# Output tiles of a fused attention and maxout kernel divided in two, with a new order of work

## The chip, the cores and the metric

The kernel runs on one core of one Trainium2 chip. Time is device time in microseconds of one execution; several executions give a median. The core has five engines with a queue each: PE (matrix multiply), ACT and DVE (elementwise, both can read the matmul results), POOL (elementwise, and here the issuer of nearly all loads) and SP (the issuer of stores). Matmul results lie in PSUM, which has eight banks of 128 partitions by 512 float32.

## The reference

Eight batches of eight heads go through an attention with 32 memory slots, and the result goes through a maxout layer.

```python
# q, k, v: (8, 8, 576, 64); phi: (8, 8, 576, 32)
a = softmax(phi, axis=2)                      # over the 576 positions
k_m = einsum('bhsm,bhsd->bhmd', a, k)
v_m = einsum('bhsm,bhsd->bhmd', a, v)
attn = softmax(q @ k_m^T / 8, axis=-1)        # over the 32 slots
x = (attn @ v_m)                              # to (4608, 512)
h = max(x @ w1, x @ w2, x @ w3)               # w1, w2, w3: (512, 768)
out = h @ w_out                               # w_out: (768, 512), out: (4608, 512) float32
```

## The kernel before, in words

**The algebra.** `x` is never formed. Per batch, `v_m` is folded into the weights: `wp = v_m (w1 - w3 | w2 - w3)` and `wp3 = v_m w3 w_out`. Then `h = w3-part + max(0, attn wp_1, attn wp_2)`, so a tile of the output is six matmuls of the hidden part with `w_out` and two of `attn` with `wp3`.

**Orders by hand.** Nothing is scheduled by a tool at build time: a string of tokens (line 602 on) is walked, and each token `n@b` issues one piece of work for batch `b`. Each engine runs its instructions in exactly that order. A `!` swaps which engine, ACT or DVE, copies the result out of PSUM. A second string (line 145) gives in order the PSUM bank that each piece takes, one digit for each; pieces that need two banks take the digit and the next one up. Semaphores hold an instruction until its inputs are there and its bank has been read.

**The tokens, per batch.**

| token | what it does | engines |
|---|---|---|
| L0, L1, L2, L3 | load phi, k, v, q (line 575) | POOL issues, DMA moves |
| r0, r1 | pack k, v into one buffer (line 102) | POOL |
| E | exp of phi (line 232) | ACT |
| B | `a^T (k, v, 1)`, 72 small matmuls (line 245) | PE |
| N, K | divide by the sum, transpose (lines 269, 299) | DVE, PE, copy on DVE or ACT |
| Q0, Q1 | transpose q (line 313) | DVE |
| S | scores and their exp (line 327) | PE, ACT |
| a, s, c, m, X | softmax over slots: transpose, sum, reciprocal, multiply, transpose back | DVE, POOL for m |
| D0, D1, D2, D3 | fold a block of 512 weight columns; D3 is `wp3` (line 427 on) | PE, copy on ACT or DVE |
| F0 to F11 | hidden tile: four matmuls 128x288; an even one is copied with max(0, .), the odd one behind it is joined by max on DVE (line 463) | PE, ACT, DVE |
| T0 to T4 | output tile, 128 rows by 512: eight matmuls, a copy, a store (line 495) | PE, ACT or DVE, SP |
| V0, V1, V2 | `w1 - w3`, `w2 - w3` in place, once (line 215) | DVE |

T4 exists for odd batches alone: its 128 rows are the last 64 of the batch before and the first 64 of this one. Its six matmuls with `w_out` span all 128 columns of the array; the two with `attn` become four narrow ones (128x64), two for either batch, since `wp3` differs.

**Shapes on the PE.** F, T, K and the warm-up matmuls use the whole 128x128 array. B and D use tiles of 64x32, S tiles of 32x32, the narrow part of T4 tiles of 128x64.

**Depth of buffers.** phi and q: two tiles each. k and v: two each. `wp`, `attn`, the hidden tile: two each. The output tile: six. So the load of k for batch b + 2 waits for the pack of batch b, and a load of q for b + 2 for the transposes of b.

**Around batch 2.** In the old order B@2 comes after the tiles T3@0, T0@0, T1@0, T2@0 and all twelve F@1; then D3@1, N@2, Q1@2, T0@1, K@2, T2@1, Q0@2, S@2.

Of the kernel before, what the change touches and what calls it, by code (L numbers as in the profile page):

```python
# [15 lines left out]
def kernel(  # L16
# [138 lines left out]
    def one_bank():  # L155
        return psum[:, int(next(banks))]
# [306 lines left out]
    def ffn1(b, n, swap):  # L463
        s = st[b]
        ft, w = n // 2, n % 2
        if b // 2 not in hts:
            hts[b // 2] = work.tile([P, FT, 2 * S], BF16, name="hT")
        hT, attn = hts[b // 2], attns[b // 2]
        acc = two_banks()
        for g in range(NG):  # L470
            for h in range(2):
                c0 = (b % 2) * S + h * SH
                nc.tensor.matmul(  # L473
                    acc[:, h, 0:SH],
                    lhsT=wps[b][:, g, w * DF + ft * P : w * DF + (ft + 1) * P],
                    rhs=attn[:, g, c0 : c0 + SH],
                    start=(g == 0),
                    stop=(g == NG - 1),
                )
# [15 lines left out]
    def ffn2(b, t, swap):


        hT, attn = hts[b // 2], attns[b // 2]
        c0 = S - HP if t == 4 else (b % 2) * (S + HP) + t * P
        if b == B - 1 and t == 3:  # L500
            return ffn2_last(b, c0)
# [9 lines left out]
        for g in range(NG):  # L511
            if t < 4:
                nc.tensor.matmul(  # L513
                    po,
                    lhsT=attn[:, g, c0 : c0 + P],
                    rhs=wp3s[b][:, g, :],
                    start=False,
                    stop=(g == NG - 1),
                )
            else:  # L520
                for u in range(2):
                    nc.tensor.matmul(  # L522
                        po[HP * u : HP * (u + 1)],
                        lhsT=attn[:, g, c0 + HP * u : c0 + HP * (u + 1)],
                        rhs=wp3s[b - 1 + u][:, g, :],
                        start=False,
                        stop=(g == NG - 1),
                        tile_position=(0, HP * u),
                    )
# [70 lines left out]


    for w in """
        E@0 H0@0 H2@0 L3@0 Z25@0 B0@0 I@0 N0@0 Z2@0 K0@0! Q0@0 Q1@0 Z9@0 S@0 Z2@0 M0@0 M1@0
        R0@0 Y2@0 G0@0 R1@0 W0@0 Y3@0 W1@0 W2@0 Z6@0 O1@0 H3@0 O3@0 O2@0 H1@0 X1@0 B1@0 X0@0 N1@0
        K1@0 O0@0 Y0@0 D1@0! D0@0! D3@0 F8@0 F10@0 F2@0 V0@0 F6@0 F0@0! Y1@0 D2@0 D4@0 F4@0
# [5 lines left out]
        X1@2 D0@2 T3@1 Q0@3 L3@4 X0@2 Q1@3 T1@1 F0@2 F4@2 F8@2 F6@2 F9@2 E@3 F7@2 r1@3 F5@2  # L611
        F10@2 F1@2 B@3 L1@4 D3@2 N@3 L0@5 F2@2 F11@2 E@4 F3@2 L1@5 K@3 r1@4 L2@5 T2@2! S@3 T3@2
        a0@3 s0@3 c0@3 m0@3 D0@3 D2@3 a1@3 s1@3 c1@3 X0@3 D1@3! Q0@4 m1@3 T1@2 L3@5 L2@6 T0@2!
        X1@3 F10@3 r0@4 F2@3 F4@3 E@5 Q1@4 r0@5 F5@3 F3@3 L1@6 F8@3 B@4 N@4 D3@3 F9@3 F6@3
        F11@3 L0@6 K@4 F0@3 F7@3 F1@3 S@4 a0@4 T4@3! s0@4 a1@4 D0@4 c0@4 s1@4 r1@5 c1@4 D3@4
        m0@4 X0@4 Q0@5 T0@3! D1@4! D2@4 B@5 T3@3 m1@4 X1@4 L0@7 F10@4 Q1@5 N@5 F8@4 K@5 F6@4
        F9@4 S@5 F7@4 L3@6 F2@4 F4@4 a0@5 L1@7 a1@5 F0@4 s0@5 r1@6 F3@4 D0@5 r0@6 s1@5 c1@5 E@6
        D3@5 m1@5 c0@5 F1@4 T1@3 L2@7 F11@4 L3@7 E@7 F5@4 m0@5 B@6 D1@5! D2@5 X1@5 N@6 T2@3!
        X0@5 F6@5 F8@5 Q0@6 Q1@6 K@6 F4@5 F9@5 S@6 F7@5 r0@7 a0@6 F2@5 a1@6 s0@6 c0@6 F0@5
        F10@5 m0@6 F1@5 s1@6 c1@6 F11@5 F5@5 T0@4! F3@5 X0@6 T2@4! r1@7 D0@6 D1@6! Q0@7 B@7  # L620
# [37 lines left out]
```

## Time and profile before

| | us |
|---|---|
| median of 3 runs | 165.57 (165.14 to 166.01) |
| the profiled execution | 165.42 |
| its span | 163.70 |
| PE busy | 153.0 |
| ACT busy | 100.5 |
| DVE busy | 90.4 |
| POOL busy | 69.7 |
| loads by POOL's queue, share of 16 DMA engines over the span | 68.7% |

Starts and durations are counted from the start of the span. An idle time is named with what ended it. A matmul's duration in the trace is that of its pipeline: 128x512 shows 380 ns, while one starts every 216 ns; 128x288 shows 286 ns and starts every 123. Some matmul records are missing: of 210 matmuls of line 504 the trace holds 193, and a missing one looks like idle time.

### The profile page before, as it was taken

To read this page: it belongs to the slowest core of one execution; us is meant where nothing else is said; L and a number is where in the kernel's file an instruction comes from. 1 tells how busy PE (TensorE), PEld (TensorE's weight loads), DVE (VectorE), ACT (ScalarE), POOL (GpSimd) and SP (SyncE) were. 2 spreads that over 40 slices of the span, in tenths; PEclk is the share of its full clock that TensorE was granted. 3 is DMA by queue.
4 is the path that set the end of the run, shared out by engine and by line. 5 is a ranking of instruction groups with operands and counts; after the bars stand their busy time and mean duration, and the time that the engine had idled before them with its cause. 6 is when DMAs were issued, how large, how long until landed. Compare 5 with 4: busy or idle time off the path is not lost.

```text
span 163.7 us, 4819 instructions
## 1 busy us (share of the span) xinstructions
PE 153.0 (93%) x2060; PEld 85.5 (52%) x2080; DVE 90.4 (55%) x181; ACT 100.5 (61%) x151; POOL 69.7 (43%) x72
## 2 busy tenths in 40 slices
PE   7987798999898999999999999999999999999990
PEld 2442444664376436753673575576553467744450
DVE  2023703898837765759399759879749228810000
ACT  4205335935496488778885989994658976323320
POOL 7275215100698276838939976755403200000000
PEclk9999999999999999999999999999999999999999
DMA  5999999999999999999999999997313230014333
GB/s 155 156 207 200 197 210 213 277 208 208 259 307 241 209 257 364 277 216 286 258 265 206 233 351 266 175 235 157 130 70 125 73 128 0 0 68 180 141 128 130
DMA packets 21974, 31.77 MB, mean 194 GB/s; under 512 B 1216, under 2 KB 16576, under 8 KB 21952
## 3 DMA queue, kind: packets, MB, share of 16 engines
q0 software_dynamic: 16080, 21.43, 68.7%
q1 hardware_dynamic: 5728, 9.90, 17.2%
q8 instruction: 16, 0.26, 0.6%
q10 hardware_dynamic: 144, 0.13, 0.2%
q14 instruction: 6, 0.05, 0.1%
HBM read 39.32 MB, written 9.44 MB: 298 GB/s over the span
## 4 chain that ended last, share of the span: by engine, by line
PE 65%; DMA 28%; POOL 2%; issue 2%; ACT 1%; POOLq 0%; ACTq 0%
PE psum L504 25%; PE psum L473 22%; DMA ph<-in_phi_dram 15%; DMA w_sb<-in_moe_w_dram 9%; PE psum L513 7%; DMA kvo<-in_k_dram 4%; PE psum L447 4%; PE psum L256 3%; PE psum L340 1%; POOL kvo L97 1%; PE psum L522 1%; PE psum L545 1%; ACT e L236 1%; PE psum L305 1%; POOL wo_sb L123 0%
## 5 line engine op out<-in xcount | busy, mean ns | idle before, releaser
L504 PE MATMUL psum<-wo_sb,hT 128*128 128x512 bf16 x193 | 49.7, 380 | 1.4 <-issue 0.6
L473 PE MATMUL psum<-attn,wp 128*128 128x288 bf16 x384 | 50.5, 286 | 0.1
L486 DVE TENSOR_TENSOR hT<-psum,h 128x576 bf16<-128x576 f32 x48 | 34.2, 749 | 18.2 <-PE psum L473 12.0
L473 PEld LDWEIGHTS <-wp 128*128 128x128 bf16 x384 | 36.7, 98 | 13.2 <-issue 1.9
L179 ACT COPY ot<-psum 128x512 f32<-128x512 f32 x35 | 20.7, 591 | 32.1 <-PE psum L513 25.2
L504 PEld LDWEIGHTS <-hT 128*128 128x128 bf16 x210 | 19.2, 98 | 24.1 <-issue 4.3
L103 POOL COPY kvr<-kvo 128x2304 bf16<-128x2304 bf16 x12 | 25.4, 2114 | 14.3 <-DMA kvo<-in_k_dram 7.9
L179 ACT CAST wp<-psum 128x1024 bf16<-128x1024 f32 (+1 forms) x31 | 29.3, 996 | 3.0 <-PE psum L447 2.1
L177 ACT ACTIVATE h<-psum 128x576 bf16<-128x576 f32 x47 | 28.4, 659 | 3.2 <-PE psum L473 3.1
L416 POOL TENSOR_TENSOR t<-t,sm 128x576 bf16<-128x576 bf16 x14 | 16.1, 1157 | 25.2 <-DVE sm L411 25.1
L513 PE MATMUL psum<-wp,attn 128*128 128x512 bf16 x62 | 18.4, 379 | 0.0
L166 PE MATMUL psum<-warm 128*128 128x512 bf16 x42 | 12.4, 450 | 1.4 <-DVE warm L135 1.2
L320 DVE STREAM_TRANSPOSE qT<-qq 128x576 f32<-128x576 f32 x16 | 11.7, 747 | 1.5 <-DMA qq<-in_q_dram 1.5
L349 ACT ACTIVATE e<-psum 128x576 bf16<-128x576 f32 x16 | 9.6, 652 | 3.8 <-PE psum L340 3.8
L236 ACT ACTIVATE e<-ph 128x1152 bf16<-128x1152 f32 (+1 forms) x9 | 9.6, 1065 | 2.6 <-DMA ph<-in_phi_dram 2.4
L402 DVE TENSOR_REDUCE sm<-t 128x18 f32<-128x576 bf16 x14 | 10.3, 738 | 0.2
L97 POOL DMA_DIRECT2D kvo<-in_v_dram x9 | 6.7, 747 | 7.2 <-PE psum L256 4.1
L513 PEld LDWEIGHTS <-attn 128*128 128x128 bf16 x62 | 6.1, 98 | 7.1
L394 DVE STREAM_TRANSPOSE t<-e 128x288 f32<-128x288 f32 x14 | 6.3, 464 | 6.2 <-ACT e L349 6.1
L562 DVE COPY ot<-psum 128x256 f32<-128x256 f32 x1 | 0.4, 425 | 15.4 <-PE psum L553 15.4
L256 PEld LDWEIGHTS <-e 64*32 64x32 bf16 x720 | 6.9, 90 | 3.4 <-issue 2.0
L166 PEld LDWEIGHTS <-warm 128*128 128x128 bf16 x44 | 4.6, 111 | 7.4 <-issue 3.5
(58 smaller groups left out, 116.4 us busy)
## 6 DMA issues: line engine op xcount, KB each, us to landing
out_dram<-ot SPq DMA_DIRECT2D x35, 256.0 KB, 5.5
qq<-in_q_dram POOLq DMA_DIRECT2D x8, 576.0 KB, 12.6
ph<-in_phi_dram POOLq DMA_DIRECT2D x7, 576.0 KB, 15.1
kvo<-in_k_dram POOLq DMA_DIRECT2D x7, 576.0 KB, 13.9
kvo<-in_v_dram POOLq DMA_DIRECT2D x7, 576.0 KB, 16.6
w_sb<-in_moe_w_dram POOLq DMA_DIRECT2D x3, 768.0 KB, 15.0
wo_sb<-in_moe_w_out_dram POOLq DMA_DIRECT2D x1, 768.0 KB, 10.7
ph<-in_phi_dram SPq DMA_DIRECT2D x2, 288.0 KB, 2.9
```

Source lines behind the costliest of these rows:

```text
L103: nc.gpsimd.tensor_copy(out=kvrs[b % 2][:, :, :, D * i : D * (i + 1)], in_=kvos[b % 2][:, 1 - i])
L166: nc.tensor.matmul(po[:, 0:BANK], lhsT=warm[:, 0:P], rhs=warm, start=True, stop=True)
L177: nc.scalar.activation(out=out_, in_=in_, func=AF.Relu)
L179: nc.scalar.copy(out=out_, in_=in_)
L236: nc.scalar.activation(out=s["e"][:, js], in_=loaded[b]["ph"][:, js], func=AF.Exp)
L256: nc.tensor.matmul(kvp[M * j : M * (j + 1), a, 0:nd], lhsT=s["e"][r, j, c, :], rhs={None: lambda: kvr[r, j, c, 0:nd], 0: lambda: k_and_one ...
L320: nc.vector.transpose(out=s["qT"][:, j].rearrange("p j c r e -> p (j c r e)").bitcast(FP32), in_=loaded[b]["q"][:, j].rearrange("p j c d - ...
L416: nc.gpsimd.tensor_tensor(out=t, in0=t, in1=s["sm", g].unsqueeze(2).to_broadcast([P, S // HP, R, 2]), op=ALU.mult,)
L473: nc.tensor.matmul(acc[:, h, 0:SH], lhsT=wps[b][:, g, w * DF + ft * P : w * DF + (ft + 1) * P], rhs=attn[:, g, c0 : c0 + SH], start=(g == ...
L486: nc.vector.tensor_tensor(out=hT[:, ft, (b % 2) * S : (b % 2 + 1) * S].rearrange("p (h n) -> p h n", h=2), in0=a, in1=s["h1", ft], op=ALU.max,
L504: nc.tensor.matmul(po, lhsT=hT[:, fc, c0 : c0 + P], rhs=wo_sb[:, fc, :], start=(n == 0), stop=False,)
L513: nc.tensor.matmul(po, lhsT=attn[:, g, c0 : c0 + P], rhs=wp3s[b][:, g, :], start=False, stop=(g == NG - 1),)
```

## The change

Three things change in the code, and with them both strings.

- A new token P issues the head of an output tile: its bank is taken, and the first three of the six matmuls with `w_out` run. The token T of the same tile later issues the other three and the two with `attn`, without taking a bank. 22 tiles are divided so; T4 and the last tile are not.
- In T4 the four narrow matmuls come first and open the accumulation, and the six wide ones follow and close it.
- The subtraction of `w3` is cut into the same four pieces as before, but one token issues one piece (V0, V1, V2, V4), where V1 issued two.
- The order of the tokens and the swaps are new behind D2@0; up to there they are the same. The banks are new throughout.

```diff
+    HEAD = 3
...
     def w_diff(n):
 
-        c, end = n * BANK, (n + 1) * BANK
-        while c < end:
-            e = min(end, (c // DF + 1) * DF)
-            nc.vector.tensor_tensor(
-                out=w12[:, :, c:e],
-                in0=w12[:, :, c:e],
-                in1=w_sb[:, :, 2, c % DF : c % DF + e - c],
-                op=ALU.subtract,
-            )
-            c = e
+        lo, end = FIRST[n]
+        nc.vector.tensor_tensor(
+            out=w12[:, :, lo:end],
+            in0=w12[:, :, lo:end],
+            in1=w_sb[:, :, 2, lo % DF : lo % DF + end - lo],
+            op=ALU.subtract,
+        )
...
+    heads = {}
+
+    def ffn2_head(b, t):
+
+        hT = hts[b // 2]
+        c0 = (b % 2) * (S + HP) + t * P
+        po = heads[b, t] = one_bank()
+        for n in range(HEAD):
+            fc = fts[b][n]
+            nc.tensor.matmul(
+                po,
+                lhsT=hT[:, fc, c0 : c0 + P],
+                rhs=wo_sb[:, fc, :],
+                start=(n == 0),
+                stop=False,
+            )
...
     def ffn2(b, t, swap):
...
-        po = one_bank()
-        for n, fc in enumerate(fts[b]):
+        po = heads[b, t] if (b, t) in heads else one_bank()
+
+        if t == 4:
+            for g in range(NG):
+                for u in range(2):
+                    nc.tensor.matmul(
+                        po[HP * u : HP * (u + 1)],
+                        lhsT=attn[:, g, c0 + HP * u : c0 + HP * (u + 1)],
+                        rhs=wp3s[b - 1 + u][:, g, :],
+                        start=(g == 0),
+                        stop=False,
+                        tile_position=(0, HP * u),
+                    )
+        for n in range(HEAD if (b, t) in heads else 0, FT):
+            fc = fts[b][n]
             nc.tensor.matmul(
                 po,
                 lhsT=hT[:, fc, c0 : c0 + P],
                 rhs=wo_sb[:, fc, :],
-                start=(n == 0),
-                stop=False,
+                start=(n == 0 and t < 4),
+                stop=(n == FT - 1 and t == 4),
             )
...
+            "P": lambda: ffn2_head(b, i),
```

The part of the order from batch 1's first B to the end of batch 2's scores, old and new, and the stretch around K@5 in the new one:

```diff
-        L0@1 V1@0 F1@0 E@1 F3@0 L1@1 F5@0 F9@0 F7@0 L3@1 F11@0 B0@1 T3@0 N0@1 K0@1! L2@1 Q1@1
-        L2@2 L1@2 Q0@1 L0@2 V2@0 T0@0! L3@2 S@1 T1@0 a0@1 s0@1 c0@1 m0@1 B1@1 N1@1 a1@1 L1@3
-        K1@1 s1@1 D0@1 D1@1! D2@1 c1@1 m1@1 X0@1 L3@3 r1@2 X1@1 T2@0! L2@3 F6@1 F10@1 F7@1 F2@1
-        F3@1 F4@1 F0@1 r0@2 E@2 F5@1 F1@1 F11@1 L0@3 L0@4 F8@1 L2@4 F9@1 B@2 D3@1 N@2 Q1@2
-        T0@1! K@2 T2@1! r0@3 Q0@2 S@2 a0@2 a1@2 s1@2 c1@2 m1@2 T4@1! D1@2! s0@2 D2@2 c0@2 m0@2
+        N1@0 K1@0 O0@0 Y0@0 D1@0! D0@0! D3@0 F8@0 F10@0 F2@0 V0@0 F6@0 F0@0! Y1@0 D2@0 L0@1
+        V2@0 L1@1 D4@0 V1@0 L3@1 F4@0 F3@0 L2@1 L1@2 F1@0 L2@2 F7@0 F5@0 F9@0 F11@0 P0@0 E@1
+        B0@1 N0@1 T3@0 K0@1! Q0@1 Q1@1 L0@2 T0@0! S@1 L3@2 P1@0 V4@0 B1@1 a0@1 T1@0 s0@1 L3@3
+        N1@1 c0@1 L2@3 a1@1 s1@1 K1@1 c1@1 m0@1 P2@0 X0@1 D1@1 D0@1 m1@1 D2@1 X1@1 T2@0! L1@3
+        r0@2 F2@1! F10@1 F0@1! F4@1 F8@1 F5@1 r1@2 F6@1 L0@3 E@2 F9@1 F11@1 L0@4 L1@4 F1@1 F7@1
+        P2@1 F3@1 B@2 N@2 D3@1 P3@1 P0@1 K@2! Q0@2 Q1@2 T0@1! S@2 a0@2 s0@2 c0@2 T4@1! m0@2
...
+        F8@3! F3@3 E@4 F4@3 F9@3 F5@3 F0@3 F7@3 B@4 D3@3 N@4 F1@3 P1@3 K@4 L1@6 L0@6 T1@3! r1@5
+        E@5 S@4 D2@4 L2@6 a0@4 T4@3! r0@5 s0@4 L0@7 a1@4 P0@3 D1@4! B@5 s1@4 c1@4 D0@4 L1@7
+        c0@4 Q1@5 m1@4 T0@3! N@5 Q0@5 K@5 P2@3 L2@7 X1@4 m0@4 S@5 X0@4 T2@3! F0@4 F2@4 a0@5
...
-        F9@6 F1@6 F3@7 T0@6! T0@7! T3@5 T2@7! T2@6! T1@6 T1@7 T3@6 T4@7! T3@7
+        P2@6 F1@7 F6@7 F7@7 T2@6 F4@7! T3@6! F8@7 T0@6! T1@6 F9@7 F5@7 F3@7 P0@7 T1@7! T0@7
+        T2@7 T4@7! T3@7
```

The string of banks changes with it:

```diff
-            00224460026701101401264026402640264026452063420643064206420642064562074206742064
-            20642064201640264102640264026402640264072406247026402640264024602406520462046204
-            62704267402640264124602416420642064206420642067676767670
+            60606026024506010445024062406246024602434403424206026420462406240723043240604602
+            46026402645260502624620640264024601642102461462624604624260462045260024062404206
+            12640264014206502402605220462406420462036040432402677670
```

More of the change, by code (lines that the diff above doesn't have):

```diff
@@ L493 @@
     osts = {}
[L495 to L501, printed above, removed]
-        po = one_bank()
-        for n, fc in enumerate(fts[b]):
+    heads = {}
[5 more added lines that the diff above has]
+            fc = fts[b][n]
             nc.tensor.matmul(
@@ L510, in ffn2 @@
             )
-        for g in range(NG):
-            if t < 4:
+    def ffn2(b, t, swap):
+        hT, attn = hts[b // 2], attns[b // 2]
+        c0 = S - HP if t == 4 else (b % 2) * (S + HP) + t * P
+        if b == B - 1 and t == 3:
+            return ffn2_last(b, c0)
+        po = heads[b, t] if (b, t) in heads else one_bank()
[19 more added lines that the diff above has]
+            )
+        if t < 4:
+            for g in range(NG):
                 nc.tensor.matmul(
@@ L519, in ffn2 @@
                 )
[L520 to L529, printed above, removed]
         ot = opool.tile([P, DM], FP32, name="ot")
@@ L603 @@
         E@0 H0@0 H2@0 L3@0 Z25@0 B0@0 I@0 N0@0 Z2@0 K0@0! Q0@0 Q1@0 Z9@0 S@0 Z2@0 M0@0 M1@0
-        R0@0 Y2@0 G0@0 R1@0 W0@0 Y3@0 W1@0 W2@0 Z6@0 O1@0 H3@0 O3@0 O2@0 H1@0 X1@0 B1@0 X0@0 N1@0
-        K1@0 O0@0 Y0@0 D1@0! D0@0! D3@0 F8@0 F10@0 F2@0 V0@0 F6@0 F0@0! Y1@0 D2@0 D4@0 F4@0
-        L0@1 V1@0 F1@0 E@1 F3@0 L1@1 F5@0 F9@0 F7@0 L3@1 F11@0 B0@1 T3@0 N0@1 K0@1! L2@1 Q1@1
-        L2@2 L1@2 Q0@1 L0@2 V2@0 T0@0! L3@2 S@1 T1@0 a0@1 s0@1 c0@1 m0@1 B1@1 N1@1 a1@1 L1@3
-        K1@1 s1@1 D0@1 D1@1! D2@1 c1@1 m1@1 X0@1 L3@3 r1@2 X1@1 T2@0! L2@3 F6@1 F10@1 F7@1 F2@1
@@ L609 @@
-        F3@1 F4@1 F0@1 r0@2 E@2 F5@1 F1@1 F11@1 L0@3 L0@4 F8@1 L2@4 F9@1 B@2 D3@1 N@2 Q1@2
-        T0@1! K@2 T2@1! r0@3 Q0@2 S@2 a0@2 a1@2 s1@2 c1@2 m1@2 T4@1! D1@2! s0@2 D2@2 c0@2 m0@2
[L611 to L620, printed above, removed]
@@ L621 @@
-        m1@6 N@7 X1@6 T2@5! K@7 T3@4 Q1@7 S@7 a0@7 F2@6 s0@7 a1@7 s1@7 c1@7 m1@7 c0@7 F4@6
-        T4@5! D3@6 D2@7 D0@7! T0@5! D3@7 D2@6 X1@7 m0@7 D1@7! T1@4 X0@7 F6@7 F3@6 T1@5 F4@7
-        F8@7 F0@7 F5@6 F10@6 F7@7 F9@7 F10@7 F5@7 F0@6 F11@7 F6@6 F1@7 F7@6 F2@7 F8@6 F11@6
-        F9@6 F1@6 F3@7 T0@6! T0@7! T3@5 T2@7! T2@6! T1@6 T1@7 T3@6 T4@7! T3@7
+        R0@0 Y2@0 G0@0 R1@0 W0@0 Y3@0 W1@0 W2@0 Z6@0 O1@0 H3@0 O3@0 O2@0 H1@0 X1@0 B1@0 X0@0
+        N1@0 K1@0 O0@0 Y0@0 D1@0! D0@0! D3@0 F8@0 F10@0 F2@0 V0@0 F6@0 F0@0! Y1@0 D2@0 L0@1
@@ new lines @@
+        V2@0 L1@1 D4@0 V1@0 L3@1 F4@0 F3@0 L2@1 L1@2 F1@0 L2@2 F7@0 F5@0 F9@0 F11@0 P0@0 E@1
[3 more added lines that the diff above has]
+        P2@1 F3@1 B@2 N@2 D3@1 P3@1 P0@1 K@2! Q0@2 Q1@2 T0@1! S@2 a0@2 s0@2 c0@2 T4@1! m0@2
+        a1@2 s1@2 c1@2 T2@1! D2@2 Q1@3 D0@2 D1@2! T3@1 m1@2 T1@1 X1@2 r1@3 L3@4 L2@4 X0@2 L2@5
@@ new lines @@
+        Q0@3 F4@2 F6@2 F0@2 F8@2 F7@2 r0@3 F1@2 F10@2 F5@2 E@3 F9@2 F11@2 F2@2 B@3 D3@2 N@3
+        F3@2 L0@5 P3@2 K@3 P0@2 L1@5 S@3 T0@2 a0@3 r0@4 s0@3 c0@3 a1@3 s1@3 P2@2 m0@3 c1@3 D2@3
+        m1@3 D1@3! L3@5 D0@3 T3@2! Q1@4 X0@3 X1@3 T2@2! Q0@4 T1@2 F10@3! r1@4 F2@3 F11@3 F6@3
+        F8@3! F3@3 E@4 F4@3 F9@3 F5@3 F0@3 F7@3 B@4 D3@3 N@4 F1@3 P1@3 K@4 L1@6 L0@6 T1@3! r1@5
+        E@5 S@4 D2@4 L2@6 a0@4 T4@3! r0@5 s0@4 L0@7 a1@4 P0@3 D1@4! B@5 s1@4 c1@4 D0@4 L1@7
+        c0@4 Q1@5 m1@4 T0@3! N@5 Q0@5 K@5 P2@3 L2@7 X1@4 m0@4 S@5 X0@4 T2@3! F0@4 F2@4 a0@5
@@ new lines @@
+        F4@4! F6@4 r1@6 a1@5 P3@3 L3@6 D1@5! r0@6 D3@4 s1@5 D3@5! T3@3 F10@4 s0@5 c1@5 F3@4
+        F8@4 c0@5 F11@4 F1@4 F7@4 F5@4 F9@4 m0@5 P1@4 P0@4 E@6 D0@5 m1@5 X0@5 B@6 D2@5 X1@5
+        T0@4 T1@4 N@6 F6@5 F0@5 F7@5 F1@5 F4@5! Q0@6 F2@5 r0@7 F10@5 r1@7 T3@4! Q1@6 F5@5 F8@5!
+        E@7 K@6! F9@5 T2@4! F3@5 S@6 F11@5 a1@6 B@7 L3@7 D2@6 N@7 a0@6 D0@6 T4@5! s0@6 K@7 Q1@7
+        P0@5 s1@6 D1@7! D3@7 c1@6 c0@6 D0@7 Q0@7 m1@6 T0@5! m0@6 P1@5 S@7 T1@5 X1@6 a0@7 a1@7
+        P3@5 X0@6 D2@7 D1@6! s0@7 c0@7 D3@6 s1@7 T3@5! m0@7 c1@7 F6@6 P2@5 m1@7 X0@7 X1@7 F10@6
@@ L625 @@
+        T2@5! F7@6 F10@7! F4@6 F0@7! F11@6 F8@6 F11@7 F0@6! F2@6 F5@6 F1@6 F3@6 F2@7! P3@6 F9@6
+        P2@6 F1@7 F6@7 F7@7 T2@6 F4@7! T3@6! F8@7 T0@6! T1@6 F9@7 F5@7 F3@7 P0@7 T1@7! T0@7
+        T2@7 T4@7! T3@7
     """.split():
```

## The prediction

> **What bounds the kernel now.** I read the busy table and the 40 slices first, then stages, then the PE's waits, then the chain in order of time.
>
> ```profile
> span 163.7 us, 4819 instructions
> PE 153.0 (93%) x2060; PEld 85.5 (52%) x2080; DVE 90.4 (55%) x181; ACT 100.5 (61%) x151; POOL 69.7 (43%) x72
> DMA  5999999999999999999999999997313230014333
> ```
>
> ```profile
> 0.00:26.60 26.60, 22.28 (x272) 10.28 (x275) 6.79 (x20) 8.87 (x14) 12.20 (x24) 1.00 1.07 189
> 26.60:52.30 25.70, 24.30 (x409) 14.75 (x413) 19.21 (x32) 17.81 (x28) 10.90 (x11) 1.00 1.17 249
> 52.30:115.30 63.00, 62.16 (x982) 36.20 (x992) 46.84 (x98) 49.56 (x72) 43.09 (x36) 1.00 1.12 247
> 115.30:160.00 44.70, 44.27 (x408) 24.25 (x410) 17.58 (x32) 23.88 (x37) 3.46 (x4) 1.00 0.26 98
> ```
>
> The columns after the stretch are PE, PEld, DVE, ACT and POOL busy, granted clock, DMA share and GB/s. Up to 26.6 us the PE waits for weights and fills with warm-up matmuls. From 52.3 to 160.0 it lacks 1.27 us in all (63.00 - 62.16 + 44.70 - 44.27), and those are mostly missing matmul records (193 of 210 of line 504 are in the trace). So after 52.3 us time can go down only by giving the PE less to do there. The clock is 1.00 throughout.
>
> ```profile
> PE psum L305 <- DVE kvn L280: 0.9, 2, 0.4
> PE psum L256 <- ACT e L236: 0.4, 1, 0.4
> PE psum L305 <- DVE kvn L290: 0.4, 1, 0.4
> PE psum L447 <- DVE kvt L183: 0.3, 1, 0.3
> ```
>
> ```profile
> 27.17 23.86 DMA ph<-in_phi_dram
> 51.05 1.17 ACT e L236
> 52.27 0.80 PE psum L256 x69
> ```
>
> After 27 us the PE's real waits are 0.43 us at 42.75 (K1@1), 0.32 at 43.30 (the fold behind it) and 0.41 at 52.27. The last decides: phi of batch 2 lands at 51.03, its exp (E@2) takes 1.17, and B@2 starts at 52.27 however early the PE is there. The two earlier waits are therefore already paid for by it: without them the PE would wait 1.16 at 52.27.
>
> **The change part by part.** Time outside the span is 165.42 - 163.70 = 1.72 us; the profiled 165.42 is 0.15 below the median 165.57. I sum against 165.42 and add 0.15 at the end.
>
> *Same work.* The split adds no matmul: a head of 3 and a rest of 3 + 2 are the old 8. The PE has 4162 instructions in both orders. The subtraction pieces (two of 1198 ns, two of 684 ns) are the same four; they stay in the DVE order ahead of the folds that read them. Priced at nothing: DVE is at 75% in that stage.
>
> *Front.* Up to D2@0 the tokens are the same and only banks differ; the fold D1@0 still waits for w1 (landed at 26.6). Price 0.
>
> *Tile mode switches.* In the next fence, first two lines: the first matmul in another tile shape starts 0.52 us after a pair of 512 columns (56.43 to 56.95), where one of the same shape starts after 0.43 (78.58 to 79.01).
>
> ```profile
> 56.43 0.59 PE L513 MATMUL psum<-wp,attn 128*128 128x512 bf16 x2
> 56.95 0.49 PE L340 MATMUL psum<-qT,kvt 32*32 32x288 bf16 x32
> ...
> 78.58 0.59 PE L513 MATMUL psum<-wp,attn 128*128 128x512 bf16 x2
> 79.01 3.10 PE L473 MATMUL psum<-attn,wp 128*128 128x288 bf16 x24
> ```
>
> So a switch costs 0.09 us. Narrow-first moves the 128x64 group from behind six wide matmuls to before them. Counted along both orders, the PE changes shape 59 times before and 58 after: the narrow group now follows a score or a fold in three of four tiles, so it starts where the shape changes anyway. That is -0.09 us. The Trainium skill (TensorEngine Tiling (Array Packing), Tiling Modes, Key Properties) says that a change of tiling mode drains the TensorE, which would speak against narrow-first had it put the group between two wide ones. The trace agrees on the drain with 0.09 us. By that rule alone, with two switches added in each of four tiles, the sum would be +0.7.
>
> *P2@1 ahead of B@2.* Up to B@2 the new order has the same PE tokens as the old one plus the head P2@1: three matmuls of 0.216 us, 0.65 us. In the new order K1@1 has T1@0's rest (1.08 us) in front, so its 0.43 goes; the fold behind K1@1 still waits, some 0.37, because a transpose and a sum (464 + 738 ns on DVE) now stand before the copy of K1@1. The PE thus comes to B@2 at about 51.86 + 0.65 - 0.75 + 0.37 = 52.1, against 52.21 when E@2 is ready. phi of batch 2 keeps its place as third load of that batch (k and v change places ahead of it), and the first four output tiles, whose writes share the DMA engines, come before it as they did. On ACT all six even F@1 now stand before E@2, two of them moved to DVE; the last even one is through by 50.2, so E@2 starts on landing again. B@2 starts at 52.27 in both: -0.65 us, bounded by 0 (if phi lands 0.65 later, or if new waits before B@2 eat it) and -1.16 - 0.09 (if phi lands early and no wait is left).
>
> *S@2.* From B@2: 0.73, fold 0.22, switch 0.09, P3@1 and P0@1 1.30, K@2 0.17, rest of T0@1 1.08, switch 0.09: S@2 would start 3.68 after, at 55.95. q of batch 2 landed at about 54.47 (the DVE transpose starts at 54.49); two transposes of 747 ns end at 55.98, and 0.06 to the PE make 56.04: +0.09 us, up to +0.5 if that load is late. Before, the same stretch was a microsecond longer.
>
> *K@5.* Between S@4 and K@5 the PE now has fold 0.22, narrow 0.43, wide 1.29, P0@3 0.65, fold 0.22, B@5 0.73, fold 0.22, rest of T0@3 1.08 and five switches: 5.30 us. DVE must do a0, s0, a1, s1, both reciprocals, Q1@5 and N@5. In the old trace the first of these starts 0.80 after S@4's end (86.68 to 87.48) and the last reciprocal ends at 90.22, that is at +3.54; plus 0.75 for Q1@5, 1.01 for N@5 (53.46 to 54.47) and 0.06: 5.36. +0.06, up to +0.3; I take +0.1. S@5 behind it has P2@3 (0.65) as cover against 0.69 for copy and hand-over: +0.05.
>
> *Banks.* A head holds its bank until its tile is done, so F tiles turn over three pairs instead of four. Counted along both orders, 14 tokens in the new one start 0.98 us (one 0.96) of PE work after the end of the even F that held their bank; in the old one none follows an even F by less than 1.07. Needed: ACT starts 0.32 us after the start of the last of four matmuls in the tightest rows, the copy takes 0.66, the hand-over 0.06: 1.04; there are 0.12 + 0.98 = 1.10. Margin 0.06 us if ACT is free, so I take 0 and keep as ends -0 and 14 x 0.1 = +1.4 (ACT late by 0.16 each time). The Trainium skill (PSUM — Partial Sum Buffer, Summary: rules for kernel authors) tells authors to evacuate promptly because PSUM is tight. A head does the contrary, for 1.9 to 8.3 us of PE work. By that rule the sum ends near the +1.4, which is a rival below.
>
> *Loads.* k, v and q of later batches change places on POOL's queue; v of batch 3 now stands before m0@1 and holds it until B1@1 is done, some 0.4 us, which reaches the PE only as about 0.1 at the first F@1, ahead of B@2. v of batch 4 is issued some 10 us later than the 53.25 of before; it should land near 77, with B@4 at about 87 and a pack of 2.1 between: 8 us of cover. q of batches 6 and 7 come last; before, the last landed at 115.3 and its scores began near 124, now near 129. Price 0.
>
> *Tail.* The last 3.7 us (a copy and two half-tile writes) are the same. Heads and F@7 now run into the last tiles, but the last five are still T1, T0, T2, T4, T3 of batch 7 with writes 1.1 to 1.7 us apart. Price 0.
>
> Sum: -0.65 - 0.09 + 0.09 + 0.10 + 0.05 + 0.05 (small bank waits in F@2) = -0.45: 164.97 for a profiled run, 165.1 as a median.
>
> **The rivals.** (1) *Bank turn-over, slower.* If ACT comes over 0.06 us late at the 14 tight turns, each miss is PE idle time, since nothing lies between F tokens. For it: ACT copies of F come in runs (0.54 us apart, against 0.49 on the PE), and the margin is a fourteenth of the need. Against: in the new order heads and DVE copies stand between. At 0.1 each: 165.1 + 1.4 = 166.5. It beats the gain once the mean miss is over 0.035 us. (2) *No gain.* phi of batch 2 lands 0.65 later, or new waits before B@2 (the fold at 0.37, X1@1) are 0.6 larger. Then only the switch is saved and the small waits (0.29) are paid: 165.57 + 0.20 = 165.8. For it: the DMA engines are full until 115 us and k of batch 2 is now the load ahead of v. Against: the same bytes in the same span. (3) *More gain.* phi lands by 50 us, and all waits after 27 us go: 165.57 - 1.25 = 164.3. Against: K1@1's fold still waits.
>
> **How the numbers follow.** 0.5% is 0.83 us, about what a measurement of this kernel (165.14 to 166.01) can tell from no change: faster ends at 164.74, slower begins at 166.40. Forecast 0.50, with its own range 164.7 to 165.5, of which a tenth lies under 164.74; rival 1 0.25, most of it above 166.40 once some late load adds to it; rival 2 0.10; rival 3 0.15, nearly all under 164.74. Faster 0.20, same 0.58, slower 0.22. The range 164.3 to 166.6 spans all three rivals and leaves out a tenth at the upper end and a twentieth below.
>
> **What would show it.** Right: B@2 again starts at 52.2 to 52.4 behind E@2, with almost no idle before it; line 256 waits on ACT for less than 0.15; from there the PE is as full as before and ends 0.4 to 0.6 earlier, near 159.4. Rival 1: PE idle time before F tokens, released by ACT h, of over 0.5 us between 60 and 145. Rival 2: B@2 after 52.8. The prediction falls if any single PE wait after 52 us is over 0.5 us: a score waiting for q, B waiting for a pack, or K waiting for DVE.

## The result, and the profile after

| | median us | range | executions |
|---|---|---|---|
| changed kernel | 164.06 | 163.44 to 164.65 | 9 |
| kernel before, beside it on the same chip | 165.08 | 164.47 to 166.01 | 9 |
| changed kernel, timed again later | 164.43 | 163.85 to 165.57 | 12 |
| kernel before, beside that | 165.13 | 164.59 to 166.33 | 23 |

The ratio is 0.994 (95% interval 0.9914 to 0.9965) in the first timing and 0.9962 (0.9944 to 0.998) in the second. The change makes the kernel 0.7 to 1.0 us faster, where 0.45 was forecast. The sign was right, the size about half of what came; the first median lies just under the lower end of the range (164.3), the second inside it.

The profiled executions took 165.42 us before and 163.68 after, a difference of 1.74. Not all of that is the change. The fold D1@0, which waits for w1, starts at 26.70 in the old trace and at 25.95 in the new one, and up to there both kernels run the same work. So 0.75 of the 1.74 is the moment at which a weight landed, and about 1.0 belongs to what follows. From here on a "stretch" is the time from the start of D1@0 to the end of the last matmul: 133.24 us in the trace of before that the prediction used, 132.24 in the trace of the changed kernel.

First the page of the changed kernel, its span, busy table and DMA row:

```profile
span 161.9 us, 4816 instructions
PE 151.5 (94%) x2056; PEld 85.6 (53%) x2080; DVE 106.4 (66%) x203; ACT 88.5 (55%) x129; POOL 69.6 (43%) x72
DMA  5999999999999999999999999995911330024133
```

DVE has taken 16 us and 22 instructions more, ACT 12 us and 22 fewer: the new order lets DVE copy more of the results. Of the 2080 matmul records that another trace of the same kernel holds, this one holds 2056, and a missing one looks like idle time. So the stages, and with them the waits, are best read from that second trace of the unchanged new kernel, which has all 2080 (columns as before: the stretch, PE, PEld, DVE, ACT and POOL busy, clock, DMA share, GB/s):

```profile
26.60:52.30 25.70, 25.27 (x440) 15.36 (x439) 21.48 (x35) 16.46 (x25) 11.29 (x11) 1.00 1.17 249
52.30:115.30 63.00, 63.00 (x959) 36.11 (x936) 48.57 (x97) 43.68 (x62) 41.53 (x34) 1.00 1.12 251
115.30:158.00 42.70, 42.70 (x436) 23.53 (x435) 29.14 (x52) 19.01 (x28) 4.58 (x4) 1.00 0.27 93
```

From 52.30 us on the PE is busy 63.00 of 63.00 and 42.70 of 42.70 us. That does not mean that it waits for nothing: a matmul of 512 columns is shown with 0.38 us and starts 0.22 after the one before it, so a wait of up to 0.16 is hidden under the shown duration. Distances from start to start find it. In this trace two are left behind B@2: 0.12 in F10@3 (the second half of its input, from X1@3, ends on DVE at 78.52, and its third matmul starts at 78.57) and 0.06 at S@5, which reads the copy of K:

```profile
93.10 0.81 PE L502 MATMUL psum<-wo_sb,hT 128*128 128x512 bf16 x3
93.90 0.49 PE L338 MATMUL psum<-qT,kvt 32*32 32x288 bf16 x32
```

S@5 starts 0.80 after the head in front of it; two distances of 0.216 and one of 0.309, that to another shape, are 0.74. What is left before 52.30, in the first trace of the changed kernel, is short. Two of its waits, and the start of the fold that one of them belongs to:

```profile
PE psum L303 <- DVE kvn L278: 0.4, 1, 0.4
PE psum L445 <- DVE kvt L184: 0.3, 1, 0.3
```

```profile
42.80 0.84 PE L445 MATMUL psum<-w_sb,kvt 64*32 64x512 bf16 x24 [0.29 <-DVE kvt L184]
```

The first of the two lies in the front, before D1@0. Of the three waits after 27 us that the prediction listed, K1@1's 0.43 and B@2's 0.41 are gone, and the fold's 0.32 has become 0.29. Now the place on which the prediction stood, E@2 on ACT and B@2 (line 254 now) on the PE, and the chain across it:

```profile
49.44 1.16 ACT L234 ACTIVATE e<-ph 128x1152 bf16<-128x1152 f32 x1 [0.40 <-DMA ph<-in_phi_dram]
```

```profile
50.80 0.65 PE L471 MATMUL psum<-attn,wp 128*128 128x288 bf16 x4
51.38 0.80 PE L254 MATMUL psum<-kvr,e 64*32 64x129 bf16 x72
```

```profile
50.96 0.49 PE psum L471 x4
51.45 0.73 PE psum L254 x68
```

In the old trace this chain went from the DMA of phi to ACT to B@2. In the new one it goes from the hidden tile F3@1 to B@2 on the PE alone. E@2 ends at 49.44 + 1.16 = 50.60, and B@2 starts 0.8 us later because the PE has other work until then. ACT still waits for phi; the PE no longer waits for ACT.

### The profile page after: what moved, and what is told of

It reads as the page before. It is cut to its first block, busy times and chain, and to the rows that moved or that the text cites. A ratio compares the mean times of both kernels' runs of the same rounds, so it can differ in the third digit from the quotient of the medians.

```text
span 161.9 us, 4816 instructions
## 1 busy us (share of the span) xinstructions
PE 151.5 (94%) x2056; PEld 85.6 (53%) x2080; DVE 106.4 (66%) x203; ACT 88.5 (55%) x129; POOL 69.6 (43%) x72
## 4 chain that ended last, share of the span: by engine, by line
PE 80%; DMA 10%; ACT 2%; issue 2%; DVE 2%; POOL 1%; ACTq 0%; POOLq 0%
PE psum L471 28%; PE psum L532 19%; PE psum L541 8%; PE psum L502 8%; DMA wo_sb<-in_moe_w_out_dram 7%; PE psum L445 6%; DMA kvo<-in_k_dram 4%; PE psum L254 4%; PE psum L200 3%; PE psum L338 2%; PE psum L522 1%; DVE sm L400 1%; PE psum L563 1%; ACT h L178 1%; PE psum L303 1%
## 5 line engine op out<-in xcount | busy, mean ns | idle before, releaser
L471 PE MATMUL psum<-attn,wp 128*128 128x288 bf16 x384 | 51.1, 286 | 0.1
L532 PE MATMUL psum<-wo_sb,hT 128*128 128x512 bf16 x131 | 34.1, 380 | 1.5 <-issue 1.4
L180 ACT CAST wp<-psum 128x1024 bf16<-128x1024 f32 (+1 forms) x30 | 28.2, 991 | 9.0 <-PE psum L445 7.2
L178 ACT ACTIVATE h<-psum 128x576 bf16<-128x576 f32 x35 | 21.7, 661 | 14.3 <-PE psum L471 14.1
L180 ACT COPY ot<-psum 128x512 f32<-128x512 f32 x24 | 14.2, 596 | 22.8 <-PE psum L541 13.6
L532 PEld LDWEIGHTS <-hT 128*128 128x128 bf16 x144 | 12.6, 98 | 16.7 <-issue 5.3
L502 PE MATMUL psum<-wo_sb,hT 128*128 128x512 bf16 x58 | 16.8, 379 | 0.5 <-issue 0.2
L182 DVE TENSOR_SCALAR h<-psum 128x576 bf16<-128x576 f32 x13 | 9.8, 752 | 3.2 <-PE psum L471 1.9
L111 POOL DMA_DIRECT2D qq<-in_q_dram x8 | 6.2, 774 | 12.8 <-DVE qT L318 7.6
L184 DVE COPY ot<-psum 128x512 f32<-128x512 f32 x11 | 7.5, 681 | 6.4 <-PE psum L541 4.4
```

Of the source, the lines that this page charges most:

```text
L178: nc.scalar.activation(out=out_, in_=in_, func=AF.Relu)
L180: nc.scalar.copy(out=out_, in_=in_)
L471: nc.tensor.matmul(acc[:, h, 0:SH], lhsT=wps[b][:, g, w * DF + ft * P : w * DF + (ft + 1) * P], rhs=attn[:, g, c0 : c0 + SH], start=(g == ...
L502: nc.tensor.matmul(po, lhsT=hT[:, fc, c0 : c0 + P], rhs=wo_sb[:, fc, :], start=(n == 0), stop=False,)
L532: nc.tensor.matmul(po, lhsT=hT[:, fc, c0 : c0 + P], rhs=wo_sb[:, fc, :], start=(n == 0 and t < 4), stop=(n == FT - 1 and t == 4),)
```

## The experiments

Each kernel is run beside the kernel before. The times of phi's landing, of E@2 and of B@2 are given from the start of D1@0 where two runs are compared, since that start alone scattered from 25.95 to 28.18 us over 13 traces.

**1. The same two kernels again.** Two more traces of the kernel before and one more of the changed kernel, with no edit.

> The kernel before, unchanged, for a second trace. In the first two traces the fold D1@0 starts at 26.70 (before) and 25.95 (after), and phi of batch 2 lands 24.33 us behind that start before and 23.47 behind it after. Theory A (the lateness of phi before belonged to that one execution): the landing comes 23.4 to 24.0 behind D1@0 here, and the wait of B@2 for E@2 is under 0.3 us. Rival B (the old order of loads or stores makes phi late): again 24.2 to 24.5 behind, wait 0.35 to 0.5. In either case the waits for K1@1 (0.43) and the fold behind it (0.32) are there again. If the start of D1@0 differs by some tenths from 26.70, the front is what scatters between executions.

> The kernel before, unchanged, a third trace, for what scatters in it. Two traces have phi of batch 2 landing at 51.03 and 50.30 us, the six of other kernels with the new order 49.42 to 50.50. Theory A (that landing scatters by 1 to 1.5 us from execution to execution whatever the order): 49.5 to 51. K1@1's waits of 0.43 and 0.32 are there in any case, and B@2's wait is what lies between E@2's end and 25.15 us behind D1@0: 0 to 0.4. Rival B (the old order itself is late): over 50.9.

> The changed kernel, unchanged, for a second trace and a narrower interval. By the two traces the stretch from D1@0 to the last matmul took 133.24 us before and 132.24 after; idle time in it was 1.24 and 0.49. Theory A: the stretch is 132.2 to 132.4 again, the ratio 0.994 +- 0.001 (1.0 us of 165), and phi lands 23.3 to 24.0 behind D1@0. Rival B (half of the measured gain was a lucky front): ratio 0.996 to 0.998.

| trace | time | stretch | phi lands, absolute (from D1@0) | E@2 ends | B@2 starts | B@2 to the end |
|---|---|---|---|---|---|---|
| before | 165.42 | 133.24 | 51.03 (24.33) | 25.51 | 25.56 | 107.67 |
| before, second | 166.08 | 134.29 | 50.30 (24.02) | 25.34 | 25.93 | 108.36 |
| before, third | 165.20 | 133.12 | 50.58 (24.04) | 25.22 | 25.28 | 107.85 |
| after | 163.68 | 132.24 | 49.42 (23.47) | 24.65 | 25.43 | 106.81 |
| after, second | 164.38 | 132.12 | 50.50 (23.73) | 24.91 | 25.31 | 106.81 |

Three things follow. The stretch is 0.88 us or more shorter in both traces after than in any of the three before. Behind B@2 it is 0.86 shorter against the first trace and 1.04 against the third. And the wait for E@2, on which the forecast was built, is not a fixed part of the old kernel: it was 0.41 in one trace, 0.12 in another, and in the second trace of before it was absent, since another wait had come first. There the second of two weights landed late (the PE's waits, then its timeline):

```profile
PE psum L447 <- DMA w_sb<-in_moe_w_dram: 0.8, 1, 0.8
PE psum L473 <- issue: 0.5, 1, 0.5
PE psum L305 <- DVE kvn L280: 0.9, 2, 0.4
PE psum L447 <- DVE kvt L183: 0.3, 1, 0.3
```

```profile
30.99 0.30 PE L447 MATMUL psum<-w_sb,kvt 64*32 64x256 bf16 x8 [0.85 <-DMA w_sb<-in_moe_w_dram]
...
52.21 0.80 PE L256 MATMUL psum<-kvr,e 64*32 64x129 bf16 x72
```

The 0.85 at D2@0 pushed the PE back, so E@2 (50.45 to 51.62 in that trace) was through before B@2 at 52.21. The 0.5 of line 473 is a gap in front of F2@5 at 110.03, where the start waits for DVE's maximum of an earlier hidden tile. In the first trace F2@5 starts 0.05 after that maximum has ended, here 0.65 after; why stays open. In that trace phi landed 24.02 after D1@0, at the border between the two theories, which decides nothing; the third, with 50.58, lies in the scatter that its theory A gave.

The old order also has a stall in T4@3 that the prediction did not count. In the trace that it used, these are the six wide matmuls of that tile on the PE, and their weight loads:

```profile
86.71 1.63 PE L504 MATMUL psum<-wo_sb,hT 128*128 128x512 bf16 x5
```

```profile
86.62 0.84 PEld L504 LDWEIGHTS <-hT 128*128 128x128 bf16 x5 [0.21 <-issue]
87.75 0.10 PEld L504 LDWEIGHTS <-hT 128*128 128x128 bf16 x1 [0.30 <-issue]
```

One of the six matmuls has no record. The second trace of before has all six of that tile:

```profile
86.64 1.74 PE L504 MATMUL psum<-wo_sb,hT 128*128 128x512 bf16 x6
```

The last weight load starts at 87.75, 0.30 after the one before it has ended, and 0.42 after DVE has finished the hidden tile F1@3 that it reads (87.33). The fourth wide matmul starts at 87.36 and the fifth at 87.75, 0.40 after it where 0.22 is the rule: 0.18 us lost. In the other two traces of before the same two start 0.51 and 0.57 apart: 0.29 and 0.35 lost (six in a row without a hole show 1.46 us, not 1.74). The 380 ns that the trace gives a matmul cover this hole almost wholly in the first trace, so its list of waits does not name it. In the new order nothing like it is left behind B@2; the largest wait there is the 0.12 in F10@3.

**2. The division without heads.** The new order and banks, but each head issues no matmul and T does all six.

```diff
-    HEAD = 3
+    HEAD = 0
```

> The changed kernel with heads of no matmul: a head token still takes its bank, and all eight matmuls run at the tile's own token; order and banks are as changed, and the result is the same. Theory A (the heads are cover, put where a result would not be back yet): each place where only a head stands between a copy and its reader loses up to 0.65 us: B0@1 behind its load 0.6, B1@1 behind its load 1.0, D1@1 behind K1@1 0.6, K@2 (two heads gone, N@2 takes 1.0) 1.0, S@3 0.6, K@3 and K@4 0.5 each, S@5 0.6, D1@7 0.5, D0@5 0.6, F1@7 0.6, some of it given back later: +4 to +8 us against the changed kernel, 168 to 172. Rival B (the order without the division gives the gain): within 0.5 us of the changed kernel.

Measured: 173.80 us (173.51 to 174.05), ratio 1.0522 (1.0493 to 1.0551) to before, so 9.4 us over the second timing of the changed kernel, and more than the 168 to 172 that were expected. Its stretch is 141.61. Some of the PE's waits:

```profile
PE psum L338 <- DVE kvt L184: 1.3, 2, 0.6
PE psum L303 <- DVE kvn L288: 1.2, 4, 0.4
PE psum L303 <- DVE kvn L278: 1.0, 2, 0.6
PE psum L445 <- DVE hT L484: 0.9, 1, 0.9
PE psum L254 <- ACT e L347: 0.8, 1, 0.8
```

The idle time lies in 20 places and comes to 7.9 us, against 0.4 in the changed kernel. They are the places where the PE waits for DVE or ACT within a batch's chain: scores (line 338) and folds (445) behind the copy of K, transposes K (303) behind the divisions N, B (254) behind ACT. In the changed kernel the matmuls of a head stand before such places. So the new order is built on the heads, and neither half of the change can be judged without the other.

**3. The head P2@1 back behind B@2.** The changed kernel, with P2@1 and its bank moved five tokens later.

```diff
-  P2@1 F3@1 B@2 N@2 D3@1 P3@1 P0@1 K@2!
+  F3@1 B@2 N@2 D3@1 P3@1 P2@1 P0@1 K@2!
```

> The changed kernel with the one head P2@1 moved from before B@2 to behind P3@1, a few tokens later; nothing else. The prediction's largest term was 0.65 us for this head standing ahead of B@2. In the two traces of the changed kernel B@2 starts 25.43 and 25.31 us behind D1@0, while E@2 ends 24.65 and 24.91 behind it. Theory A (E@2 no longer sets the start, phi lands early enough): B@2 starts at 24.8 to 25.0, waits at most 0.25 for E@2, and the stretch from D1@0 to the last matmul stays at 132.1 to 132.5; time within 0.3 us of the changed kernel. Rival B (the prediction's: B@2 is held at about 25.5 by phi whatever the PE does): a wait of 0.6 or more, stretch 132.8, time 0.5 to 0.65 longer.

Measured: 164.77 us (164.28 to 165.63), ratio 0.9985 (0.995 to 1.0019); stretch 132.57, 0.33 to 0.45 more than in the two traces after. E@2 on ACT, B@2 on the PE, and DVE beside them, in its timelines:

```profile
49.68 1.16 ACT L234 ACTIVATE e<-ph 128x1152 bf16<-128x1152 f32 x1
```

```profile
49.77 1.90 PE L471 MATMUL psum<-attn,wp 128*128 128x288 bf16 x12
51.78 0.80 PE L254 MATMUL psum<-kvr,e 64*32 64x129 bf16 x72
```

```profile
49.55 3.41 DVE L484 TENSOR_TENSOR hT<-psum,h 128x576 bf16<-128x576 f32 x5 [0.22 <-PE psum L471]
```

E@2 ends at 50.84 and B@2 starts 0.9 after it. So without that head in front B@2 is still not held by phi. What comes back instead are two short waits, shown as 0.11 us before F3@1 and 0.11 before B@2; from start to start they are 0.27 and 0.18. Both are released by DVE's maxima of hidden tiles, and DVE runs five of these without a pause from 49.55 to 52.96 (the third row): the PE is there before the bank is read out. Together they are 0.45, as much as the stretch has grown (0.33 to 0.45). So the head in front of B@2 is worth some 0.4 us, all of it as cover for these two waits and none for phi.

**4. K1@1 earlier.** The one real wait left, 0.29 at the fold behind K1@1, was to be taken away by putting K1@1 in front of DVE's a1@1 and s1@1.

```diff
-  N1@1 c0@1 L2@3 a1@1 s1@1 K1@1 c1@1 m0@1 P2@0
+  N1@1 c0@1 L2@3 K1@1 a1@1 s1@1 c1@1 m0@1 P2@0
```

> The changed kernel with the token K1@1 moved ahead of a1@1 and s1@1, so that DVE copies K1@1's transpose before the transpose and the sum of the softmax (about 1.2 us of DVE work) instead of behind them; nothing moves on the PE. It takes away the one wait of any size that is left after 26 us, 0.29 us at D1@1. Theory A (nothing holds B@2 any more, each idle stretch of the PE is time): B@2 starts 0.2 to 0.3 earlier relative to D1@0 than the 25.43 of the changed kernel, and the time falls by 0.2 to 0.3 us. Rival B (B@2 is held by E@2, as the prediction had it): the 0.29 returns as a wait of B@2 for E@2, time unchanged.

Measured: 164.86 us (164.31 to 165.41), ratio 0.9984 (0.9964 to 1.0003), so 0.4 slower than the changed kernel beside it. Its timeline on the PE and on DVE:

```profile
43.05 0.88 PE L445 MATMUL psum<-w_sb,kvt 64*32 64x512 bf16 x24
44.95 0.41 PE L471 MATMUL psum<-attn,wp 128*128 128x288 bf16 x2
46.08 1.63 PE L471 MATMUL psum<-attn,wp 128*128 128x288 bf16 x12 [0.72 <-DVE attn L422]
```

```profile
42.51 0.22 DVE L184 COPY kvt<-psum 128x128 bf16<-128x128 bf16 x1 [0.41 <-PE psum L303]
42.65 0.47 DVE L392 STREAM_TRANSPOSE t<-e 128x288 f32<-128x288 f32 x1
...
45.57 0.45 DVE L422 STREAM_TRANSPOSE attn<-t 128x288 f32<-128x288 f32 x1
```

The fold no longer waits. But the copy of K1@1 now stands in DVE's queue before the PE has done K1@1, and DVE waits for it, 0.41 us, with the whole softmax of the second half behind it (transpose, sum, reciprocal, multiply, transpose back). Its last step X1@1 ends 19.57 us after D1@0 (at 46.02) instead of 19.00, and F2@1, the first tile to read it, waits 0.72. The wait of 0.29 hid in part the end of that chain: in the changed kernel the same matmul already starts 0.10 late, under the shown durations. The wait moved, and grew. It did not go to B@2, as rival B had it, but to the first reader of X1@1, which the prediction names in its rival 2 and not in its sum.

**5. The narrow matmuls last.** The changed kernel, with T4's narrow group behind the wide one as it was before.

```diff
-        if t == 4:
-            for g in range(NG):
-                ...
         for n in range(HEAD if (b, t) in heads else 0, FT):
...
-                start=(n == 0 and t < 4),
-                stop=(n == FT - 1 and t == 4),
+                start=(n == 0),
+                stop=False,
...
+        if t == 4:
+            for g in range(NG):
+                ...
+                        start=False, stop=(g == NG - 1)
```

> The changed kernel with the narrow matmuls of T4 last again, as before the change. Counted along the order, the PE then changes tile shape 61 times instead of 58. At 0.093 us each the stretch from D1@0 to the last matmul grows by 0.28, to 132.4 to 132.5, and so does the time (0.2%, less than three rounds can tell). Rival: narrow-first also lets the tile wait less for what its wide matmuls read (its hidden tile is done later than its wp3), then the growth is 0.5 or more and a wait shows at the first wide matmul of T4.

Measured: 164.68 us (164.03 to 165.5), ratio 0.9981 (0.995 to 1.0011); stretch 132.43, against 132.18 as the mean of the two traces after: +0.25. At T4@1 the PE now goes from scores to wide, to narrow, and to wide again:

```profile
55.08 0.47 PE L338 MATMUL psum<-qT,kvt 32*32 32x288 bf16 x32
55.49 1.47 PE L521 MATMUL psum<-wo_sb,hT 128*128 128x512 bf16 x5
56.89 0.62 PE L531 MATMUL psum<-wp,attn 128*64 128x512 bf16 x4
57.44 0.82 PE L521 MATMUL psum<-wo_sb,hT 128*128 128x512 bf16 x3
```

This order has three changes of tile shape more than the changed kernel, and 3 x 0.09 is 0.27. The size agrees with the price of 0.09 that the prediction read from one pair of rows, though 0.25 is only about twice what two traces of the same kernel differ by. The distances in this trace say it more firmly: where a matmul of 512 columns in the full shape is followed by another shape and no wait, which is so 18 times, the next one starts 0.31 after it, against 0.22 in the same shape.

**6. The loads in their old order.** In the changed kernel k of batch 2 goes back behind v.

```diff
-  L2@1 L1@2 F1@0 L2@2 F7@0
+  L2@1 F1@0 L2@2 L1@2 F7@0
```

> The changed kernel with the loads of batch 2 in the old order: v, k, phi instead of k, v, phi. phi of batch 2 landed 24.33 and 24.02 us behind D1@0 in two traces of the kernel before, and 23.47, 23.73, 23.23 in three with the changed loads. Theory A (the order of k and v makes the difference, k can be issued some 4 us earlier than v): 24.0 to 24.4 here, and B@2 waits for E@2 up to 0.3. Rival B (something else in the order, or chance): 23.2 to 23.8, no wait.

Measured: 164.99 us in one execution, with D1@0 late at 27.13; the stretch is 132.33. phi lands 23.01 after D1@0, not later than in the two traces after (23.47 and 23.73). So nothing speaks for the order of k and v as what made phi early (one trace; the old orders of experiments 7 and 8 also have phi early, at 22.71 to 23.48). What changes is the wait in front of B@2:

```profile
51.86 0.65 PE L471 MATMUL psum<-attn,wp 128*128 128x288 bf16 x4
52.69 0.80 PE L254 MATMUL psum<-kvr,e 64*32 64x129 bf16 x72 [0.17 <-POOL kvr L104]
```

B@2 waits 0.17 us for POOL's pack of k, which is loaded second here instead of first. E@2, at 24.20 after D1@0, is done 1.4 before B@2 starts. So k's earlier place in the new order has a use, but at the pack, not at phi.

**7. Narrow matmuls first, in the old order.** All of the new code, with the old order and banks and no heads.

```diff
-  V1@0 ... V2@0
+  V1@0 V2@0 ... V4@0
```

> The old order, undivided, in the new code: the narrow matmuls of T4 first and the subtraction in four tokens, nothing else. Sixty changes of tile shape against 59: +0.09 us. Theory A: stretch from D1@0 to the last matmul as in the kernel before, 133.2 plus 0.1 and plus whatever single wait this execution has; time within 0.3 us of the kernel before. Rival (narrow-first is itself worth something, or costs it, in the old order): more than 0.5 us either way.

Measured: 165.46 us (164.85 to 166.66), ratio 1.0014 (0.9983 to 1.0045): no change that can be told. Up to B@2 this kernel gives the engines the same work in the same order as the kernel before. Here phi lands 23.08 after D1@0, E@2 ends at 24.50, and B@2 starts at 25.09 without a wait, 0.48 earlier than in the trace that the prediction used. Of that 0.38 is lost again behind B@2. There the trace shows a stall at T4@3 (line 522 is the narrow group, 532 the wide one here), larger than the old 0.18:

```profile
85.85 0.49 PE L338 MATMUL psum<-qT,kvt 32*32 32x288 bf16 x32
86.35 0.62 PE L522 MATMUL psum<-wp,attn 128*64 128x512 bf16 x4
87.57 1.24 PE L532 MATMUL psum<-wo_sb,hT 128*128 128x512 bf16 x5 [0.60 <-issue]
```

About 0.4 of the 0.60 is real: the record of the first wide matmul is missing, and by its neighbours it started at 87.35. F1@3 ends on DVE at 86.96, while the narrow group runs. With the wide matmuls first it was the fifth of them that came late; with the narrow ones first it is the first wide one, although the matmul that reads F1@3 is the sixth. In the three traces with this order the wide ones start 0.40 to 0.47 us after F1@3 is finished. Why the earlier ones are held too, no view names.

**8. One head alone, in the old order.** As 7, and the head P2@1 in front of B@2. The first of the two runs had a slow front (its clock was 0.86 between 10 and 20 us, and D1@0 began at 28.18), so it was run again.

```diff
-  F9@1 B@2 D3@1
+  F9@1 P2@1 B@2 D3@1
```

> The old order in the new code (narrow-first, four subtraction tokens) with one head alone: P2@1 directly before B@2, its rest at T2@1's place; banks of B@2, D3@1, T0@1, S@2, D1@2 and D0@2 changed to make room. Sixty changes of tile shape against 59: +0.09. By both accounts B@2's wait for E@2 (0.41 in the first trace, none in the second) is filled: from B@2 to the last matmul 107.67 - 0.65 + 0.09 = 107.1; from D1@0 to B@2 25.56 grows to 25.8 if phi is late, or by the whole 0.65 if it is not. Theory A (the gain of the change is the sum of all the idle time, of which K1@1's 0.43 and 0.32 remain here): stretch 132.9 to 133.4, time 0 to 0.4 us under that before. Rival B (this head is the gain): 0.65 or more under that before.

> The old order with one head, once more. Its first timing was 0.85 us above the kernel before, while its trace had D1@0 at 28.18, 1.5 us later than any other trace, a granted clock of 0.86 between 10 and 20 us, and one stall of some 0.5 us at 89 that no semaphore explains. Theory A (chance of the front): D1@0 at 26 to 27.2 here, stretch 132.8 to 133.0, time 0 to 0.4 us under the kernel before. Rival B (something in this kernel makes the front late): D1@0 over 27.5 again and 0.5 us or more above the kernel before.

Measured: 165.96 us (164.93 to 167.09), ratio 1.0047 (1.0016 to 1.0079), and 165.5 us (164.99 to 167.03), ratio 1.0039 (1.001 to 1.0069). Both are some 0.4% slower than before. Around B@2 the second trace does what a head in front should do:

```profile
51.14 0.81 PE L502 MATMUL psum<-wo_sb,hT 128*128 128x512 bf16 x2
51.88 0.80 PE L254 MATMUL psum<-kvr,e 64*32 64x129 bf16 x72
```

No wait for E@2; B@2 starts 25.73 after D1@0, against 25.28 to 25.93 in the three traces of before, with 0.65 more work done. But the stretches are 133.40 and 133.33, more than the 132.8 to 133.0 expected for the second: nothing was gained over the 133.12 and 133.24 of before. The waits 0.43 and 0.32 in front of K1@1 and its fold are still paid. Behind B@2 there is a head less (-0.65), but one change of shape more (0.09), S@2 now waits (0.12 as shown, 0.19 from start to start), and T4@3 loses 0.61 and 0.55 as in 7, where the first trace of before loses 0.26 (0.18, and 0.08 at its first matmul, which waits for DVE too). That leaves 0.02 and 0.08 of gain; measured are 107.67 and 107.60 against 107.67. The stretches do not show the 0.4% by which the medians are slower; that part is open. The one edit that the forecast's main term stands for is thus no gain by itself.

## Why the prediction was right or wrong

**Right: the bound.** The PE sets the time, and only PE idle time and shape changes could be gained. The complete trace of the changed kernel shows 0.4 us of idle time from D1@0 on. (The 4162 PE instructions of the prediction stand in no trace; a complete trace has 2080 matmuls and 2080 weight loads in either order.)

**Right: the switch price and the narrow group.** 0.09 us per change of shape holds: 0.31 against 0.22 at 18 places of one trace, and three changes more go with +0.25 (experiment 5). Counted in the traces, the changes are 59 before and 58 after, as predicted. The Trainium skill (TensorEngine Tiling (Array Packing), Tiling Modes, Key Properties) names the drain, and that run agrees with it; the sum of +0.7 which the prediction worked out from that rule alone did not come, because the narrow group stands where the shape changes anyway.

**Right: rival 1 was to be refused.** The 14 tight turns of a bank cost nothing that can be seen. In the second trace after, no matmul of a hidden tile behind B@2 starts more than 0.05 us late by the distances, apart from the one in F10@3, which waits for its input and not for a bank. The Trainium skill (PSUM — Partial Sum Buffer, Summary: rules for kernel authors) has authors evacuate promptly. Here 22 heads hold a bank for 1.9 to 8.3 us of PE work, no run of the changed order shows a lasting cost, and taking them away costs 9.4 us. The nearest to that rule's harm are the two waits in experiment 3, 0.45 together.

**Wrong: "B@2 starts at 52.27 in both".** This is the step that failed. It took phi's landing at 51.03 as a fixed time. Over 13 traces of these kernels phi landed between 49.3 and 51.03; the one that the prediction read was the latest of all. Even in the six traces that have the same work up to E@2 (three of before, experiments 7 and 8) it landed 22.71 to 24.33 after D1@0. That the three of before are the three latest of all 13 from D1@0 on (24.02 to 24.33, the others up to 23.73) no run explains. In both traces after, E@2 was done 0.4 to 0.8 before B@2. Against the trace that the prediction used the balance up to B@2 is then plain: before it paid 0.43 + 0.32 + 0.41 = 1.16 of waits, after 0.29, and it does 0.65 more work, which makes 1.16 - 0.29 - 0.65 = 0.22 earlier. Measured from D1@0, B@2 starts 0.13 and 0.25 earlier (25.43 and 25.31 against 25.56). The term was -0.65 and should have been near -0.87. But the 0.41 in it is luck of that trace: where phi is early the old order does not pay it either. The third trace of before, which waits 0.12, comes to B@2 at 25.28, and experiment 7, without that wait, at 25.09, both ahead of the changed kernel. This is rival 3's mechanism (phi is early, the waits go) with one wait left, and its time, 164.3, is the nearest of the four to what was measured; phi landed by 50, as rival 3 had it, in one of the two traces after (49.42 and 50.50).

**Wrong: the four new waits.** S@2 (+0.09), K@5 (+0.10), S@5 (+0.05) and the bank waits in F@2 (+0.05) were priced at 0.29 together. By the distances three of them are in neither trace; S@5 is there in both, with 0.06. Each was worked out from rows of another order, with ACT and DVE as loaded as they were there, and came out at 0.1 us or less on the side of a loss. For S@2 the landing of q was again taken as fixed, at 54.47; it landed at 52.84 and 53.94. A margin that thin is a coin, and four coins were counted as four losses; one fell so.

**Wrong: "those are mostly missing matmul records".** They were, but 0.18 us of T4@3 was not (0.29 and 0.35 in the other two traces), and one trace of before has another 0.51 at F2@5. The prediction took every gap after 52 us for missing records and so had no old stall to remove there. Behind B@2 the difference should have been 0.65 + 0.09 + 0.18 = 0.92, and 0.86 was measured (107.67 - 106.81). Smaller waits nearly cancel: three of 0.08 in the old order, 0.12 and 0.06 in the new one.

**The sum mended.** 0.22 up to B@2 and 0.92 behind it are 1.14 by its terms, against a measured 1.00 to 1.12 in the stretches (133.24 against 132.24 and 132.12). Without a wait for E@2 in the old order, 0.73 would be left (1.14 - 0.41). By the medians it is 0.7 in one timing and 1.02 in the other, both with an interval that excludes no change.

**The baseline.** The 165.57 that the forecast was moved to came from three executions; with 9 to 23 the same kernel had medians of 165.08, 165.11, 165.13 and 165.16. That alone put the predicted 165.1 some 0.4 too high, as much as the whole forecast gain.

## What to carry to other kernels

A wait that ends on a load is a draw, not a time: before a forecast is built on "held until 52.27", look at several traces, and price the term for an early and a late landing. Half a tile of output is good cover for the gaps in a chain, but here only in an order written around it; one head alone in the old order gained nothing. To look for stalls on a full PE, use distances from start to start: the shown duration hides up to 0.16 us of a wait, and a missing record looks like one of 0.22. And a copy put earlier in an in-order queue makes all that stands behind it wait for the copy's input.

## What the runs showed of the hardware

- The landing of one load in a saturated stretch (DMA busy nine tenths from 5 to 110 us) scattered by 1.7 us over 13 traces of these kernels, and the start of D1@0, which waits for w1, by 2.2 us (25.95 to 28.18). From D1@0 on, executions of one order agreed much better (132.24 and 132.12; 133.24 and 133.12, with one 134.29 where two further stalls were seen).
- A matmul that only waited for its input started 0.06 us after it was ready (B@2 behind E@2 in the first trace of before); F2@5 did so after 0.05 in that trace and after 0.65 in the second. In T4@3 with the narrow group first, the wide matmuls started 0.40 to 0.47 us after the end of the hidden tile that only the last of them reads, and in the old order the weight load that reads it started 0.42 to 0.60 after (three traces). A late weight load there seems to hold matmuls ahead of it; the runs show the delay, not its mechanism.
